# An attention and GEGLU block on one core: the output projection in plain F32 products with other load orders, and a third of the normalised input loaded into both halves of its tile at block changes

## The chip, the cores and the metric

The kernel runs on one core of one Trainium2 chip. The metric is the device time of one execution in microseconds (us). The engines are named as in the profile: PE (TensorE, matrix products; PEld is its weight load), DVE (VectorE), ACT (ScalarE), POOL (GpSimd) and SP (SyncE), which here issues every transfer.

## The reference

```
xn = layernorm(x)                                   # x: 2048 rows of 576, F32
q, k, v = xn @ wqkv                                 # 32 heads of 18
s = softmax(q k^T / sqrt(18)) v @ wo                # wo: 576 x 576
g = silu( (gelu(xn @ w_gate) * (xn @ w_up)) @ w_down )   # 4608 hidden
out = x + s * g
```

## The kernel before

[...] To keep the precision, an operand is split into a high part (rounded to fp32r) and a low part (what is left), and a product is the sum of high by high, high by low and low by high. The transposes of the prologue and the accumulation of the attention (L848) use plain F32 operands.

The order of the work on PE is written out by hand for the whole kernel; that of the other engines is given by a scheduler, except where `keep` (keep in program order) fixes it, and in the tail, where ACT, DVE and POOL follow the program as well. SP issues the transfers in its order, and eight of them can be open: a transfer is issued when the eighth before it has landed.

The 2048 rows of x are worked off in four blocks of 512 (`NB`, `TB`).

*Prologue* (to about 200 us). Layer norm, transposes and the projections to q, k and v for four blocks. Beside the last of them `wo` is read in five pieces, split by POOL (`split_wo`, L313) and stored in two parts, high and low, in the DRAM tile `wos` (`store_wo`, L321). The high and low parts of the transposed xn are stored in `xhs`.

*Main part* (to about 2456 us). The FFN runs in sections. A section forms one gate and one up product for 128 hidden channels and a block: 54 matmuls (L427) with the weights `wh`, `wl` (five buffers each, split from `raw`) and the block's `xd`. Each of the 18 rounds of a block has two sections, and a `down` of 42 matmuls (L538), which multiplies the activations (`ah`, `al`, their high and low parts, made by ACT and POOL from the sums `h`) by `T`, the prepared down weights, and adds the products to `M`. Between the matmuls of a section stand those of the attention: the scores for the maxima (L779, DVE), the scores again (L831), their exponential on ACT (L832) and the accumulation (L848).

*Block changes* (about 726, 1336 and 1942 us). A block's `xd` are six tiles of 128 partitions, `xd0` and `xd1` (the high and the low part) for each of three thirds k of xn's channels, XG = 3 groups of 64 channels to a tile. Both 64-partition halves of a tile hold the same data, since gate products use one half of the array and up products the other. In the last section of a block (`new` in `section`, L571) `load_xd` (L139) loads the first halves of thirds 0 and 1 by hooks in the section, and those of third 2 after it; `copy_xd` (L148) fills the second halves: those of `xd0` on ACT, those of `xd1` on POOL. POOL's order before is: the copies of third 0, the activation's sums, `ah`, `al`, the copies of third 1, `wh` and `wl`, the copies of third 2. `finish` puts the sums and cuts of that section into the tenth hook of the next one (`behind`, L640).

*Tail* (from about 2456 us). Five FFN sections and three downs are left, and the output projection in 16 steps, one for each 128 rows (`groups`). The order on PE: three sections, down 0, four steps, a section, three steps, down 1, two steps, a section, two steps, down 2, five steps. A step (`step`) is:

- `project`: attention rows by `wo`, five row groups (`NK`, the last of 64 rows) and two halves of 288 columns, in a PSUM slot of `ring`, which has three slots that sections, downs and steps share. With `oh`, `ol` and `woh`, `wol` these are 28 matmuls (L991).
- `multiply` (L995): the gate `yy` by the product, plus `xx`, and the store of the output rows.
- `split_o` for the step after the next: `oh` on ACT (L972), `ol` and a 64-partition piece of `oh` on DVE (L973, L974). After the last group of block 0 or 1 it also issues `load_o(b + 2)`, which reads the attention rows of a later block into the slots of `KA` that block b leaves (`OTS`).
- `gate` for the step after the next: tanh on ACT (L982) and one DVE operation (L983) on the FFN rows `ys`.
- `load_xy` four steps ahead, and two of the four `T` pieces of the next down, where there are any (`pieces`).

The attention rows that are not yet normalised at the end of the main part go through `load_scale`, `scale` (POOL, L705) and `store_scale` into `on`, one after the other. `XX` has three buffers and four more (`xxs`) later, `YY` has four.

```
for k in range(2):
    step()
load_raw(first + 4)
for k in range(2):
    step()
h, end = last_section("ring")
```

## Time and profile before

| | us |
|---|---|
| median of 3 runs | 2597.23 (2595.16 to 2600.65) |
| the profiled execution, its own time | 2595.73 |
| its span | 2593.9 |
| its granted PE clock | 0.995 |
| PE busy | 2554.1 |
| DVE busy | 2111.7 |
| POOL busy | 1599.7 |
| ACT busy | 1468.6 |

A row of a group reads: line, engine, operation, tiles (out<-in), shapes and count, then busy time and the mean of one in ns, then the idle time ahead of it and what ended it. Rows of the chain of waits are: start, length, engine, tile and line, with "x42" for 42 instructions in a row. A row of waits is: who waited, for whom, the time in all, how often, the longest. PE matmuls are pipelined, so the pace of a run of them (its length by its count) says more than the mean of one. The clock is that granted to PE, in parts of full speed.

```profile
PEclk9999999999999999999999999999999999999998
```

This line of the page is the granted clock in 40 equal slices of the span, in tenths of full speed.

### The profile page before, as it was taken

To read this page: it belongs to the slowest core of one execution; us is meant where nothing else is said; L and a number is where in the kernel's file an instruction comes from. 1 tells how busy PE (TensorE), PEld (TensorE's weight loads), DVE (VectorE), ACT (ScalarE), POOL (GpSimd) and SP (SyncE) were. 2 spreads that over 40 slices of the span, in tenths; PEclk is the share of its full clock that TensorE was granted. 3 is DMA by queue.
4 is the path that set the end of the run, shared out by engine and by line. 5 is a ranking of instruction groups with operands and counts; after the bars stand their busy time and mean duration, and the time that the engine had idled before them with its cause. 6 is when DMAs were issued, how large, how long until landed. Compare 5 with 4: busy or idle time off the path is not lost.

```text
span 2593.9 us, 52857 instructions
## 1 busy us (share of the span) xinstructions
PE 2554.1 (98%) x20548; PEld 1847.5 (71%) x20548; DVE 2111.7 (81%) x2399; ACT 1468.6 (57%) x1769; POOL 1599.7 (62%) x1679
## 2 busy tenths in 40 slices
PE   9999999999999999999999999999999999999988
PEld 8887766666666777666666676666666666676778
DVE  5325888888888888888878988888887888887377
ACT  3224366666666666555566655555566555556521
POOL 2115588888888855666667665555557655556641
PEclk9999999999999999999999999999999999999998
DMA  8865455555565566666666666666557665554683
GB/s 264 266 237 147 109 166 152 167 164 161 167 188 164 165 170 165 159 165 166 167 174 172 168 167 162 161 160 157 155 151 213 163 156 150 153 155 134 187 255 126
DMA packets 407880, 442.87 MB, mean 171 GB/s; under 512 B 106700, under 2 KB 286412, under 8 KB 407632
## 3 DMA queue, kind: packets, MB, share of 16 engines
q1 hardware_dynamic: 407632, 439.50, 61.6%
q8 instruction: 163, 2.67, 0.4%
q14 instruction: 85, 0.70, 0.1%
HBM read 344.12 MB, written 95.26 MB: 169 GB/s over the span
## 4 chain that ended last, share of the span: by engine, by line
PE 92%; DVE 2%; DMA 2%; POOL 1%; ACT 1%; issue 1%; SPq 1%; POOLq 0%; DVEq 0%; ACTq 0%
PE pg L427 27%; PE acc L848 17%; PE py L538 14%; PE pe L831 9%; PE pm L779 9%; PE po L187 7%; PE pu L427 7%; PE py L525 1%; PE po L991 1%; DMA raw<-in_B_w_up_dram 0%; DMA wol<-wos 0%; DVE mx L781 0%; DMA KA<-on 0%; PE pt L248 0%; DMA yy<-ys 0%
## 5 line engine op out<-in xcount | busy, mean ns | idle before, releaser
L832 ACT ACTIVATE pT<-pe 128x1024 f32<-128x1024 f32 x1024 | 1049.0, 1027 | 586.0 <-PE pe L831 551.1
L781 DVE TENSOR_REDUCE mx<-pm 128x2 f32<-128x1024 f32 x1024 | 1220.5, 1224 | 176.6 <-PE pm L779 161.8
L427 PE MATMUL pu<-xd,wh 64*128 64x512 f32 x2538 | 927.5, 397 | 6.5 <-POOL xd L153 4.9
L427 PE MATMUL pg<-xd,wh 64*128 64x512 f32 x2538 | 926.0, 396 | 1.9 <-ACT t L440 1.9
L427 PEld LDWEIGHTS pg<-xd,wh 64*128 64x128 f32 x2538 | 468.6, 185 | 123.7 <-issue 57.0
L427 PE MATMUL pg<-xd,wl 64*128 64x512 f32 x1269 | 496.4, 391 | 1.2 <-POOL wl L117 1.2
L427 PE MATMUL pu<-xd,wl 64*128 64x512 f32 x1269 | 495.9, 391 | 0.0
L427 PEld LDWEIGHTS pu<-xd,wh 64*128 64x128 f32 x2538 | 468.5, 185 | 24.4 <-POOL xd L153 5.7
L110 POOL TENSOR_SCALAR wh<-raw 128x384 fp32r<-128x384 f32 x402 | 215.4, 537 | 437.4 <-PE pu L427 333.4
L848 PE MATMUL acc<-pT,VS 128*32 128x512 f32 x4096 | 466.0, 595 | 0.0
L112 POOL TENSOR_TENSOR wl<-raw,wh 128x384 fp32r<-128x384 f32 x402 | 413.4, 1031 | 28.6
L779 PE MATMUL pm<-KA,QT 64*128 64x512 f32 x2048 | 416.5, 394 | 5.6 <-ACT pT L832 3.6
L831 PE MATMUL pe<-QT,KA 64*128 64x512 f32 x2048 | 412.5, 392 | 2.2 <-DVE mx L781 1.9
L538 PE MATMUL py<-T,ah 128*128 128x288 f32 x1876 | 385.9, 301 | 9.9 <-DVE yy L1000 7.0
L545 DVE TENSOR_TENSOR M<-py,M 128x576 f32<-128x576 f32 x448 | 338.8, 758 | 31.2 <-PE py L538 18.5
L538 PEld LDWEIGHTS py<-T,ah 128*128 128x128 f32 x1876 | 302.0, 190 | 65.9 <-issue 61.5
L456 POOL TENSOR_TENSOR al<-h,ah 128x512 fp32r<-128x512 f32 (+1 forms) x142 | 292.8, 2062 | 52.6 <-ACT ah L453 42.5
L848 PEld LDWEIGHTS acc<-pT,VS 128*32 128x32 f32 x4096 | 120.3, 109 | 276.5 <-issue 229.5
L538 PE MATMUL py<-T,al 128*128 128x288 f32 x938 | 277.8, 296 | 0.0
L831 PEld LDWEIGHTS pe<-QT,KA 64*128 64x128 f32 x2048 | 194.3, 184 | 113.0 <-DVE mx L781 26.2
L427 PEld LDWEIGHTS pg<-xd,wl 64*128 64x128 f32 x1269 | 234.4, 185 | 38.4 <-POOL wl L117 2.0
L427 PEld LDWEIGHTS pu<-xd,wl 64*128 64x128 f32 x1269 | 234.7, 185 | 8.3
(156 smaller groups left out, 2908.4 us busy)
## 6 DMA issues: line engine op xcount, KB each, us to landing
T<-ts SPq DMA_DIRECT2D x98, 576.0 KB
KA<-qk SPq DMA_DIRECT2D x768, 72.0 KB
T<-ts SPq DMA_DIRECT2D x98, 432.0 KB
raw<-in_B_w_gate_dram SPq DMA_DIRECT2D x144, 288.0 KB
raw<-in_B_w_up_dram SPq DMA_DIRECT2D x144, 288.0 KB
ts<-T SPq DMA_DIRECT2D x36, 576.0 KB
VS<-vs SPq DMA_DIRECT2D x128, 152.0 KB
qk<-t SPq DMA_DIRECT2D x72, 256.0 KB
```

What stands on the lines that cost most here:

```text
L110: first = nc.gpsimd.tensor_scalar(hi, raw, 1.0, 1.0, op0=ALU.mult, op1=ALU.mult)
L112: keep(nc.gpsimd.tensor_tensor(lo, raw, f(hi), op=ALU.subtract))
L187: nc.tensor.matmul(o, st, m, start=(i == 0), stop=(i == len(terms) - 1))
L427: nc.tensor.matmul(o, w[1 + wp][k][rr, c, :], xd[k][xp][rr, c, :], start=(i == 0), stop=(i == len(terms) - 1))
L456: keep(two.tensor_tensor(lo, raw, f(hi), op=ALU.subtract))
L538: nc.tensor.matmul(py[:, t, 0:DC], h[:, i, tt], T[:, w, k], start=n == 0, stop=n == 2)
L545: nc.vector.tensor_tensor(M[:, m], py[:, :, 0:DC], M[:, m], op=ALU.add)
L779: nc.tensor.matmul(pm[:, a], QS[u, r][rr, t * P:(t + 1) * P], KS[(u * NA + c) % KB][r][rr, :], start=True, stop=True)
L781: return nc.vector.tensor_reduce(MX[u][:, 2 * r:2 * r + 2, t, c], pm, axis=AX.X, op=ALU.max)
L831: nc.tensor.matmul(pe[:, a], KS[(u * NA + c) % KB][r][rr, t * P:(t + 1) * P], QS[u, r][rr, :], start=True, stop=True)
L832: nc.scalar.activation(PT[u, kt][:, 2 * r:2 * r + 2, :], pe, AF.Exp, scale=SCALE)
L848: nc.tensor.matmul(ACC[u][32 * a:32 * a + 32, :], VS[(u * NA + c) % VB][:, v:v + 32], pt[:, a, :], start=first, stop=last, skip_group_chec ...
```

## The change

*Output projection.* `split_wo`, `store_wo` and `wos` go. In the tail `wo` is read as it is into one F32 tile, and `project` multiplies the F32 rows in `KA` by it: ten products per step, five row groups by two halves. `split_o` goes. `XX` has five buffers (and the four `xxs`), `YY` seven; `load_x` and `load_y` ask for rows nine and seven groups ahead. The loads for the scaling are issued together, all four pieces of `T` for the next down are asked for ahead of the first step, the raw weights of the last section earlier, and `load_o(b + 2)` follows the products of the last step of block b. `gate` runs for the step after the next one, as before, with `step(False)` where a down stands between.

*Block changes.* `load_xd` takes `halves`; with 2 it issues a transfer for each half of a tile. The last third is loaded so, and its copies on ACT and POOL go. The POOL copies of thirds 0 and 1 stand together after the section, ahead of the sums; and `behind` issues sums and cuts at once, in program order, instead of in the tenth hook.

```diff
--- before.py
+++ after.py
@@ -92,7 +92,6 @@
     qk = dram.tile([2, 2 * D, S], F32, name="qk")
     vs = dram.tile([S, H, DH + 1], F32, name="vs")
     oT = dram.tile([NQ, P, S], F32, name="oT")
-    wos = dram.tile([2, D, D], F32, name="wos")
     rT = dram.tile([H, S], F32, name="rT")
     on = [dram.tile([D, TB], F32, name=f"on{b}") for b in range(NB)]
     mxT = [dram.tile([8 * QD, P], F32, name=f"mxT{i}") for i in range(2)]
@@ -136,12 +135,14 @@
         w[1].append(hi)
         w[2].append(lo)
 
-    def load_xd(b, k):
+    def load_xd(b, k, halves=1):
 
         out = []
         for i in range(2):
             t = wts.tile([P, XG, TB], F32R, name=f"xd{i}_{k}")
-            nc.sync.dma_start(f(t)[0:HR], xhs[b][i, k * XG * HR:(k + 1) * XG * HR, :].rearrange("(k p) t -> p k t", p=HR))
+            for a in range(halves):
+                nc.sync.dma_start(f(t)[HR * a:HR * a + HR],
+                                  xhs[b][i, k * XG * HR:(k + 1) * XG * HR, :].rearrange("(k p) t -> p k t", p=HR))
             out.append(t)
         return out
 
@@ -266,7 +267,6 @@
         nc.vector.memset(eps, EPS)
         for v in VN:
             nc.vector.memset(v, 1.0)
-        parts = []
         ORDER = (4, 5, 0, 1, 6, 7, 8, 2, 3)
         WQK, WV = {}, {}
 
@@ -309,18 +309,6 @@
             v = VN[2 * j + c]
             nc.scalar.activation(v[:, :, 1:DH + 1], o[:, 0:D // 2].rearrange("p (h d) -> p h d", d=DH), AF.Copy)
             nc.sync.dma_start(vs[t * P:(t + 1) * P, c * H // 2:(c + 1) * H // 2, :], v)
-
-        def split_wo(k):
-            n = min(P, D - k * P)
-            raw = raw_tile([P, D])
-            tc.keep_in_program_order(nc.sync.dma_start(raw[0:n], wo[k * P:k * P + n, :]))
-            hi, lo = (pro.tile([P, D], F32R, name=f"wo{i}", tag="rawp", bufs=5) for i in range(2))
-            split(hi[0:n], lo[0:n], raw[0:n])
-            return k, n, hi, lo
-
-        def store_wo(k, n, hi, lo):
-            for i, t in enumerate((hi, lo)):
-                tc.keep_in_program_order(nc.sync.dma_start(wos[i, k * P:k * P + n, :], f(t)[0:n]))
 
         NQT = 2 * D // P
         raw_v, ahead_qk, QR = [], [], []
@@ -372,10 +360,6 @@
                 if b == 0 and n in (7, 8):
                     split_wv(n - 7, raw_v[n - 7])
                 project(b, t, xt)
-                if b == NB - 1 and 2 <= n < NK + 2:
-                    store_wo(*parts.pop(0))
-                if b == NB - 1 and n < NK:
-                    parts.append(split_wo(n))
                 if n == 4 and b + 1 < NB:
                     norm(xr, b + 1)
             store_xt(b, xt)
@@ -612,11 +596,10 @@
         if g > 0 or n not in ATT:
             FF.pop("last", lambda: None)()
         if new:
-            xd.append(load_xd(b + 1, NG - 1))
-            for k in range(1, NG):
-                for i in range(XG):
-                    FF["hooks"].setdefault(7 * k + 2 * i - 5, []).append(lambda k=k, i=i: copy_xd(xd[k], 0, keep, i))
-            for k in range(NG):
+            xd.append(load_xd(b + 1, NG - 1, 2))
+            for i in range(XG):
+                FF["hooks"].setdefault(2 + 2 * i, []).append(lambda i=i: copy_xd(xd[1], 0, keep, i))
+            for k in range(NG - 1):
                 for i in range(XG):
                     copy_xd(xd[k], 1, keep, i)
             FF["xd"] = xd
@@ -638,10 +621,7 @@
             FF[ahead].setdefault(i, []).append(what)
 
         def behind(what):
-            if (n + 1) % (NR * G) == 0:
-                hook(9, lambda: what(keep))
-            else:
-                what(lambda i: i)
+            what(keep if (n + 1) % (NR * G) == 0 else lambda i: i)
 
         if g == 1 and (b, r + 1) in NEXT:
             load_rawd((r + 1) % NR)
@@ -937,64 +917,50 @@
 
 
     with tc.tile_pool(name="epi", bufs=1, reuse_waits="tile") as epi:
-        OW = [epi.tile([P, NK, D], F32R, name=name) for name in ("woh", "wol")]
-        XX = [epi.tile([P, D], F32, name=f"xx{i}") for i in range(3)]
-        YY = [epi.tile([P, D], F32, name=f"yy{i}") for i in range(4)]
-        OP = {}
+        OW = epi.tile([P, NK, D], F32, name="wo")
+        XX = [epi.tile([P, D], F32, name=f"xx{i}") for i in range(5)]
+        YY = [epi.tile([P, D], F32, name=f"yy{i}") for i in range(7)]
         groups = [(b, j) for b in range(NB) for j in range(TB // P)]
         rest, pieces = list(range(scaled, NU)), []
         pool, vec, act = nc.gpsimd, nc.vector, nc.scalar
         n = 0
 
         def load_wo():
-            nc.gpsimd.memset(f(OW[1])[HR:P, KT, :], 0.0)
-            for i, w in enumerate(OW):
-                nc.sync.dma_start(f(w)[:, 0:KT, :], wos[i, 0:R0, :].rearrange("(k p) n -> p k n", p=P))
-                for a in range(2 - i):
-                    nc.sync.dma_start(f(w)[HR * a:HR * a + HR, KT, :], wos[i, R0:D, :])
+            nc.sync.dma_start(OW[:, 0:KT, :], wo[0:R0, :].rearrange("(k p) n -> p k n", p=P))
+            nc.sync.dma_start(OW[0:HR, KT, :], wo[R0:D, :])
 
         def rows(k):
             b, j = groups[k]
             return slice(b * TB + j * P, b * TB + (j + 1) * P)
 
-        def load_xy(k):
+        def load_y(k):
+            if k < len(groups) and groups[k][0] < NB - 1:
+                nc.sync.dma_start(YY[k % len(YY)], ys[rows(k), :])
+
+        def load_x(k):
             if k < len(groups):
                 nc.sync.dma_start(XX[k % len(XX)], x[rows(k), :])
-                if groups[k][0] < NB - 1:
-                    nc.sync.dma_start(YY[k % 4], ys[rows(k), :])
-
-        def split_o(k):
-            if k >= len(groups):
-                return
-            b, j = groups[k]
-            oh, ol = OP[k] = [epi.tile([P, c, P], F32R, name=m, bufs=2) for m, c in (("oh", NK), ("ol", KT))]
-            raw = f(KA)[:, OTS[b]:OTS[b] + NK, j * P:(j + 1) * P]
-            act.activation(oh, raw, AF.Copy)
-            vec.tensor_tensor(ol, raw[:, 0:KT], f(oh)[:, 0:KT], op=SUB)
-            vec.tensor_tensor(oh[HR:P, KT, :], raw[0:HR, KT], f(oh)[0:HR, KT, :], op=SUB)
-            if b < 2 and j == TB // P - 1:
-                load_o(b + 2)
 
         def gate(k):
             if k < len(groups) and groups[k][0] < NB - 1:
-                yy = YY[k % 4]
+                yy = YY[k % len(YY)]
                 th = epi.tile([P, D], F32, name="th")
                 act.activation(th, yy, AF.Tanh, scale=0.25)
                 vec.scalar_tensor_tensor(yy, th, 1.0, yy, op0=ADD, op1=ALU.mult)
 
         def project(k):
+            b, j = groups[k]
             po = ring("po")
-            oh, ol = o = OP.pop(k)
-            terms = [(c, i, w) for c in range(KT) for i, w in ((0, 0), (0, 1), (1, 0))] + [(KT, 0, 0), (KT, 0, 1)]
             for c in range(2):
-                for m, (i, a, w) in enumerate(terms):
-                    nc.tensor.matmul(po[:, c, 0:DC], o[a][:, i, :], OW[w][:, i, DC * c:DC * c + DC], start=(m == 0),
-                                     stop=(m == len(terms) - 1))
+                for i in range(NK):
+                    rr = slice(0, P if i < KT else HR)
+                    nc.tensor.matmul(po[:, c, 0:DC], f(KA)[rr, OTS[b] + i, j * P:(j + 1) * P],
+                                     OW[rr, i, DC * c:DC * c + DC], start=i == 0, stop=i == KT)
             return po
 
         def multiply(k, po):
             b, j = groups[k]
-            xx, t = XX[k % len(XX)], YY[k % 4]
+            xx, t = XX[k % len(XX)], YY[k % len(YY)]
             t2 = t.rearrange("p (c d) -> p c d", c=2)
             if b < NB - 1:
                 vec.scalar_tensor_tensor(t2, t2, 0.25, po[:, :, 0:DC], op0=ALU.mult, op1=ALU.mult)
@@ -1005,16 +971,20 @@
             vec.tensor_tensor(xx, xx, t, op=ADD)
             nc.sync.dma_start(out[rows(k), :], xx)
 
-        def step():
+        def step(ahead=True):
             nonlocal n
             multiply(n, project(n))
-            split_o(n + 2)
-            gate(n + 2)
-            load_xy(n + 4)
+            b, j = groups[n]
+            if b < 2 and j == TB // P - 1:
+                load_o(b + 2)
             for t in pieces[:2]:
                 t()
             del pieces[:2]
+            load_y(n + len(YY))
+            load_x(n + len(XX))
             n += 1
+            if ahead:
+                gate(n + 1)
 
         def load_raw(n):
             FF["raw"][n] = load_gu(n % (NR * G))
@@ -1059,61 +1029,62 @@
         load_raw(first + 2)
         h, end = last_section("f")
         todo.pop("rec")[0]()
-        split_o(0)
+        for u in rest:
+            load_scale(u)
+        load_wo()
+        for k in range(2):
+            load_y(k)
+        load_raw(first + 3)
         end()
         sums_a(1, h, vec)
         cut_a(1, h, act, vec)
-        load_wo()
-        load_scale(rest[0])
-        load_xy(0)
-        load_xy(1)
-        load_raw(first + 3)
         h, end = last_section("ring")
-        split_o(1)
         end()
-        scale(rest[0])
-        store_scale(rest.pop(0))
-        if rest:
-            load_scale(rest[0])
-        load_xy(2)
+        for u in rest:
+            scale(u)
+            store_scale(u)
+        for k in range(4):
+            load_x(k)
+            load_y(k + 2)
         h1, end = last_section("f")
         last_down(0)
         end()
         gate(0)
-        while rest:
-            scale(rest[0])
-            store_scale(rest.pop(0))
-            if rest:
-                load_scale(rest[0])
+        gate(1)
         sums_a(0, h, pool)
         cut_a(0, h, pool, pool)
         sums_a(1, h1, pool)
         cut_a(1, h1, pool, pool)
-        gate(1)
+        load_raw(first + 4)
         for m in ("rawd", "tsum"):
             t = ffn.tile([P, 2, D], F32, name="xxs", tag=m)
             XX.extend((t[:, 0], t[:, 1]))
-        load_xy(3)
-        for k in range(2):
-            step()
-        load_raw(first + 4)
-        for k in range(2):
+        for t in pieces:
+            t()
+        del pieces[:]
+        for k in range(4, len(XX)):
+            load_x(k)
+            if k + 2 < len(YY):
+                load_y(k + 2)
+        for k in range(4):
             step()
         h, end = last_section("ring")
         end()
-        for k in range(3):
+        for k in range(2):
             step()
+        step(False)
         last_down(1)
+        gate(n + 1)
         sums_a(0, h, pool)
         cut_a(0, h, pool, pool)
-        for k in range(2):
-            step()
+        step()
         h, end = last_section("f")
         end()
         sums_a(1, h, vec)
         cut_a(1, h, act, vec)
         for k in range(2):
             step()
+        step(False)
         last_down(2, {6: ((vec, 6, SUB, 3),), 0: ((vec, 6, ADD, 0), (pool, 5, ADD, 0), (pool, 5, ADD, 2)),
                       4: ((vec, 6, SUB, 4), (vec, 4, ADD, 2)), 1: ((pool, 5, SUB, 1), (pool, 1, SUB, 3))})
         step()
```

## The prediction

> **What bounds the kernel now.** I read the page first, for the engine that fills the span, then the last stage as a table of stretches, then its waits, and last the chain of work at the three block changes.
>
> ```profile
> span 2593.9 us, 52857 instructions
> PE 2554.1 (98%) x20548; PEld 1847.5 (71%) x20548; DVE 2111.7 (81%) x2399; ACT 1468.6 (57%) x1769; POOL 1599.7 (62%) x1679
> ```
>
> PE is busy for 98% of the span, so time is won only where PE has less to do or stops waiting. The change touches two places: the tail, in which the output projection runs, and the block changes. The table below cuts the tail at the ends of its pieces of work; its columns are the stretch and its length, then busy time (instructions) of PE, PEld, DVE, ACT and POOL, the granted clock, the DMA share and GB/s.
>
> ```profile
> core 0: us, PE busy (x) PEld busy (x) DVE busy (x) ACT busy (x) POOL busy (x), PEclk, DMA share, GB/s
> 2456.30:2475.26 18.96, 18.96 (x164) 15.20 (x163) 11.74 (x14) 4.93 (x8) 6.67 (x9) 1.00 1.06 330
> 2475.26:2481.98 6.72, 6.14 (x43) 5.71 (x43) 6.63 (x11) 1.87 (x3) 1.30 (x1) 1.00 1.01 184
> 2481.98:2502.03 20.05, 16.75 (x114) 16.35 (x113) 15.29 (x18) 4.26 (x7) 16.13 (x15) 0.91 0.53 162
> 2508.38:2521.42 13.04, 11.57 (x86) 11.29 (x85) 6.56 (x11) 3.75 (x6) 3.32 (x5) 1.00 1.08 340
> 2521.42:2536.33 14.91, 8.78 (x44) 8.00 (x43) 13.16 (x17) 2.00 (x3) 5.18 (x5) 0.77 0.66 221
> 2557.72:2569.86 12.14, 8.94 (x44) 8.15 (x43) 11.34 (x18) 0.78 (x2) 1.28 (x1) 0.72 0.30 97
> 2569.86:2589.38 19.52, 19.36 (x142) 18.57 (x140) 17.31 (x25) 4.63 (x7) 5.82 (x4) 1.00 0.22 76
> ```
>
> The chain of waits prices undisturbed work, and names what the disturbed work waited for.
>
> ```profile
> 680.02 5.78 PE py L538 x42
> 2462.79 10.42 DMA wol<-wos
> 2499.29 10.31 DMA KA<-on
> 2511.53 8.04 DMA yy<-ys
> 2536.49 7.42 PE po L991 x56
> ```
>
> A down (42 matmuls of L538) costs 5.78 us, and a step of the projection, 28 of the 56 matmuls in the last row, 3.71 us. Against these, the rows of the table in order: three sections, no loss; down 0, 6.72 − 5.78 = 0.9; four steps, 20.05 − 4×3.71 = 5.2; three steps, 1.9; down 1, 9.1; down 2, 6.4; five steps, 1.0. In all 24.5 us in which PE waited, or ran at the 0.72 to 0.91 of its clock that the waiting stretches show. The waits of PE in the tail say on whom:
>
> ```profile
> PE py L538 <- DVE yy L1000: 7.0, 3, 4.7
> PE po L991 <- DVE ol L973: 4.9, 3, 3.3
> L973 DVE TENSOR_TENSOR ol<-KA,oh 128x512 fp32r<-128x512 f32 x16 | 14.9, 933 | 2.7 <-ACT oh L972 2.7
> ```
>
> The DVE is named, but its own predecessors in the chain are DMAs: the split weights (10.42 us), a block's rows of attention (10.31 us) and the FFN rows `ys` (8.04 us). So the loss has two roots, late loads and the low parts that DVE makes.
>
> **The change, part by part.**
>
> *Tail, the products.* 28 fp32r matmuls per step go, and 10 plain F32 products of 288 columns come. Nothing in the tail of before is such a product, but the accumulation of the attention is one.
>
> ```profile
> L848 PE MATMUL acc<-pT,VS 128*32 128x512 f32 x4096 | 466.0, 595 | 0.0
> 330.46 3.57 PE acc L848 x32
> ```
>
> The program issues 2048 of these products, and the trace has 4096 records: two per F32 product. Four stand side by side in the array (128*32), so 32 records take eight turns of 3.57/8 = 0.446 us for 512 columns. In proportion to columns a record of 288 takes 0.251 us, and a step of 20 records 5.02. [...] I take the middle, 5.16, since both rows are equally near: 16×(5.16 − 3.71) = **+23.2 us**, between +21.0 and +25.4. [...]
>
> *Tail, the waits.* What goes per step is one ACT activation, and on DVE the subtraction of 0.933 us at L973 with its small neighbour: 16×0.933 = 14.9 us of DVE, which stood ahead of the multiplies that free the ring slots. PE then reads the loaded rows themselves, so the 4.9 us row disappears by construction. The 7.0 us row ends at L1000, which waits for `yy`, that is for `gate` and its load. The new order asks for `ys` rows seven groups ahead and `x` rows nine ahead. `wo` is read once in its own form, half the bytes of `woh` and `wol`, and before the second of the five sections. Walking SP's new order by estimate, with the durations above (10.4 us for a large load behind others), the weights are there at about 2472, four steps' rows of `x` and `ys` before the first step, and all `T` pieces of down 1 at about 2492. `load_o(b+2)` now stands behind the PE products of the last step of block b, because PE reads the rows directly; before, it stood behind a split done two steps earlier. It is issued some two steps later, but 33 us of PE work lie between it and its first reader for b = 1 (a section of 18.96/3 = 6.3, three steps 15.5, a down 5.8, one step 5.2), and a section more for b = 0, against 10.3 for the load. That work covers it; without the cover it would cost up to those 10.3. The tightest is the last: the rows of block 3 and the `T` pieces of down 2, at about 2553 to 2554 for a PE that gets there at 2555. I leave 1 us of waiting: **−23.5 us**, between −24.5 and −13 if one wait of the size of a load stays.
>
> *Prologue.* Five loads, ten stores and five splits on POOL go from the last token block, which lies in the third of the page's forty slices.
>
> ```profile
> PE   9999999999999999999999999999999999999988
> ```
>
> PE is full there, so I take 0: these had PE's own work as cover. Two raw loads move ahead in SP's order, into the same cover.
>
> *Block changes.* Downs stand 33.3 us apart when nothing is in the way (680.02 to 713.33). The chain at the changes:
>
> ```profile
> 713.33 5.74 PE py L538 x42
> 751.29 5.74 PE py L538 x42
> 1319.86 5.74 PE py L538 x42
> 1360.41 5.81 PE py L538 x42
> 1925.35 5.74 PE py L538 x42
> 1961.61 5.74 PE py L538 x42
> ```
>
> The pairs that hold a change take 37.96, 40.55 and 36.26: 4.7, 7.2 and 3.0 us too much. What stood in the way:
>
> ```profile
> 726.57 7.71 DMA xd<-xhs
> 734.40 1.74 POOL xd L153 x3
> 741.28 2.91 POOL al L456
> 744.25 0.62 POOL xd L153
> PE pu L427 <- POOL xd L153: 3.6, 1, 3.6
> 1349.23 0.43 PE pu L427
> 1948.49 1.16 ACT xd L151 x2
> 1952.43 1.16 ACT xd L151 x2
> ```
>
> Change 1: a POOL copy of `xd` (744.25) had to wait behind the sums and the low part `al` (2.91 us), and PE behind it. This copy is of the last third, which the DMA now writes into both halves, so it goes; I take 2.3 of the 4.7 (0.5 to 3.3), as later DVE waits stay. Change 2: PE waited 3.6 us for a POOL copy behind `al`, and then ran matmuls at 0.43 instead of 0.23 for some 6 us. POOL's new order has the copies of the first two thirds ahead of the sums, so both go: 5.2 (2.8 to 6.1). Putting `sums` and `cut` in at once, not nine hooks later, delays only what stands behind them on POOL, the `wh` and `wl` splits of the next section, which have five buffers. Change 3: six copies stand on ACT between the exponentials that PE waits for; three of 0.58 go, 1.7 us.
>
> Against this stand two more DMAs at each change, in front of the `KA`, `VS`, raw and `T` loads in SP's queue, which the next down waits for.
>
> ```profile
> 1936.00:1947.00 11.00, 11.00 (x97) 6.92 (x95) 8.82 (x10) 9.69 (x12) 6.43 (x11) 1.00 1.02 212
> 1955.00:1959.00 4.00, 4.00 (x38) 2.91 (x38) 3.60 (x4) 3.44 (x5) 3.74 (x7) 1.00 1.03 410
> SPq L869 <- DMA xd<-xhs: 1.7, 1, 1.7
> ```
>
> While `xd` goes into 64 partitions the DMA engines are full at 212 GB/s; the `T` loads into 128 get 410. A transfer of a third is 64×3×512×4 = 393 KB, 1.9 us at 212 GB/s. Two more push the queue by 3.7 us if they run one behind the other, by nothing if the two halves share the time, as 410 GB/s would allow. I take 1.5 (0 to 3.7), hidden at changes 1 and 2, and charged fully to change 3, where `T` still moves at 1959 and the down starts at 1961.61: 1.7 − 1.5 = 0.2 (−2.3 to 1.8). The sum is 2.3 + 5.2 + 0.2: **−7.7 us**, between −11.2 and −1.0.
>
> [...]
>
> *Sum.* The profiled execution took 2595.73 us with a span of 2593.9. 2595.73 + 23.2 − 23.5 − 7.7 = 2587.7. The median of the runs shown, 2597.23, lies 1.5 above this execution; with it, **2589 us**. About 5 us (0.2%) is what a measurement of this kernel can tell from no change, so under 2592 counts as faster and over 2602 as slower.
>
> **The rivals.**
>
> *A: the doubled transfers push the `T` loads past their readers.* For it: the DMA share is 1.02 to 1.03 around the change, nothing there is idle, and 2.6 us after 1959 the down begins. Against: 212 GB/s is half of what the same engines do elsewhere. The price is the block changes' lower bound, −1.0 in place of −7.7: 2589 + 6.7 = 2596.
>
> *B: the F32 weight loads show.* Place: all 320 records of the projection.
>
> ```profile
> L848 PEld LDWEIGHTS acc<-pT,VS 128*32 128x32 f32 x4096 | 120.3, 109 | 276.5 <-issue 229.5
> L248 PE MATMUL pt<-ident,xx 128*128 128x128 f32 x80 | 9.4, 273 | 1.5 <-DVE xx L230 1.5
> ```
>
> The loads that are hidden in L848 have 32 columns, those of the projection 128. The transposes of L248 load 128 columns for each record and run at 9.4/80 = 0.117 us, so that is the most a load can hold PE: 320×0.117 = +37, 2589 + 37 = 2626. It decides from (2602 − 2589)/320 = 0.04 us a record. Against: 0.117 is well under the 0.251 of a record, and the fp32r loads of 128 columns are hidden behind passes of 0.1325. [...] No row of before shows a 128-column F32 load beside a long pass.
>
> *C: the tail's waits stay in part.* SP issues in order and the DMA share of the tail's first 19 us is already 1.06 at 330 GB/s; now `wo`, `ys` and scale loads are asked for together. If one load of 10.3 us stays late, 2589 + 9.5 = 2598; if all waits stay, 2612.
>
> *That the change doesn't do what it says* can't be for the products, which are in the program; for the loads it is C.
>
> **How the numbers follow.** Forecast 0.52, with a range of its own of 2582 to 2594 (from its terms: products −2.2 to +2.2, changes −3.5 to +3); A 0.17; C 0.18, of which a third over 2602; B 0.13. Faster than 2592: five sixths of the forecast and a fifth each of A and C, 0.50. Slower than 2602: B and a third of C, 0.19. Within: the rest, 0.31. The range 2577 to 2604 takes in A and the first case of C; B and the worst of C lie above it, all terms at their best below it, together about 0.2.
>
> **What would show it.** Steps: the chain should show 20 records of the projection in 5.0 to 5.3 us; 5.9 or more speaks for B. Tail: the waits of PE there should come to about 1 us, with the granted clock at 1.00 in every stretch; a wait ended by `KA<-on` or `T` would be C. Changes: downs 35.7, 35.4 and 36.1 us apart; 37 or more at all three is A, and then the `T` loads land after the sums are done. No wait on a POOL `xd` copy may be left at change 2. The prediction is wrong as a whole if F32 records cost over 0.3 us, or if the chain of the tail still runs through DMAs.

## The result, and the profile after

The changed kernel takes 2605.07 us in the median of 15 runs (2600.45 to 2608.41) against 2597.23 for the kernel before; the ratio is 1.0026, with a 95% interval of 1.0018 to 1.0034. It is slower by some 7 us, 0.26%, and the forecast was 2589. Its profiled execution took 2601.46 us, 5.7 more than that of before.

The page first. Its columns are those of the page of before.

```profile
span 2599.7 us, 52470 instructions
PE 2574.5 (99%) x20420; PEld 1842.9 (71%) x20420; DVE 2089.4 (80%) x2367; ACT 1452.6 (56%) x1744; POOL 1581.6 (61%) x1659
```

PE is busy for 20 us more, the span is 5.8 us longer: PE waits less and has more to do. The stretches of the tail, cut at the same pieces of work, show where.

```profile
core 0: us, PE busy (x) PEld busy (x) DVE busy (x) ACT busy (x) POOL busy (x), PEclk, DMA share, GB/s
2456.57:2475.17 18.60, 18.60 (x163) 15.10 (x163) 11.29 (x13) 3.62 (x5) 7.86 (x10) 1.00 0.97 277
2480.95:2503.04 22.09, 22.09 (x83) 13.75 (x83) 15.04 (x14) 3.42 (x5) 19.09 (x17) 1.00 0.93 301
2526.35:2532.13 5.78, 5.78 (x44) 5.78 (x44) 5.67 (x8) 0.00 (x0) 1.92 (x2) 1.00 0.60 194
2566.41:2594.71 28.30, 28.22 (x101) 17.30 (x100) 15.29 (x21) 2.74 (x4) 6.98 (x4) 1.00 0.11 42
```

PE is busy for the whole of each stretch and the clock is 1.00 throughout: down 1 takes 5.78 us where it took 14.91 before. No wait is left. But five steps of the projection take 28.30 us, 5.66 each, against a forecast of 5.16 and 3.71 before. The chain of waits has all steps, in five rows:

```profile
2480.95 22.09 PE po L957 x79
2509.45 16.90 PE po L957 x60
2532.13 5.19 PE po L957 x19
2543.74 16.90 PE po L957 x60
2566.41 28.23 PE po L957 x100
```

They sum to 89.3 us; 16 steps of 3.71 are 59.4. (The change also moved one step from behind down 1 to behind the section that follows, which the description of the change leaves out: 20 and 60 records stand there.) The products cost 29.9 us more, and the tail as a whole, from the end of the last down of the main part to the last product, went from 133.1 to 138.1 us: the waits gave back 24.9.

At the block changes, the chain has the downs around each change (the first, and the second after it). The last row of a view can be cut off by its end, as x33 and the last x41 are; its start counts here.

```profile
713.91 5.74 PE py L522 x42
785.55 4.55 PE py L522 x33
1317.53 5.74 PE py L522 x42
1346.76 8.73 DMA T<-ts
1355.53 7.14 PE py L522 x41
1390.20 5.74 PE py L522 x42
1922.17 5.74 PE py L522 x42
1994.46 5.61 PE py L522 x41
```

The waits of PE for `T`, one row from a window around change 2 and one from change 3:

```profile
PE py L522 <- DMA T<-ts: 2.8, 2, 2.2
PE py L522 <- DMA T<-ts: 2.7, 2, 2.3
```

The pairs of intervals are 71.64, 72.67 and 72.29 us, against 74.46, 73.91 and 69.54 before: 2.8 and 1.2 us gained at changes 1 and 2, 2.75 lost at change 3, 1.3 in all. The waits are new: at changes 2 and 3 the down waits 0.6 and 0.4 us for its first piece of `T`, does one matmul and waits another 2.2 and 2.3 us for a later piece. And once it had waited, it ran on slowly: 41 matmuls took 7.14 us at change 2, where 42 take 5.74. The granted clock (third column from the end) tells why:

```profile
1355.50:1357.00 1.50, 1.47 (x6) 1.47 (x7) 0.00 (x0) 0.00 (x0) 0.00 (x0) 0.50 0.58 152
1357.00:1359.00 2.00, 2.00 (x11) 2.00 (x10) 1.18 (x2) 0.00 (x0) 0.61 (x1) 0.55 0.34 123
1359.00:1361.00 2.00, 2.00 (x17) 2.00 (x17) 1.76 (x3) 0.00 (x0) 1.31 (x2) 1.00 0.50 148
```

For some 3.4 us behind the wait PE had about half of its full speed, which cost another 1.4 us.

### The profile page after: what moved, and what is told of

Same layout as the page of the kernel before. It is cut to its first block, busy times and chain, and to the rows that moved or that the text cites. A ratio compares the mean times of both kernels' runs of the same rounds, so it can differ in the third digit from the quotient of the medians.

```text
span 2599.7 us, 52470 instructions
## 1 busy us (share of the span) xinstructions
PE 2574.5 (99%) x20420; PEld 1842.9 (71%) x20420; DVE 2089.4 (80%) x2367; ACT 1452.6 (56%) x1744; POOL 1581.6 (61%) x1659
## 4 chain that ended last, share of the span: by engine, by line
PE 95%; DMA 2%; DVE 1%; POOL 1%; SPq 1%; ACT 1%; issue 0%; POOLq 0%; DVEq 0%; ACTq 0%
PE pg L411 26%; PE acc L828 17%; PE py L522 15%; PE pe L811 9%; PE pm L759 9%; PE pu L411 7%; PE po L188 7%; PE po L957 3%; PE py L509 1%; DMA T<-ts 1%; DMA raw<-in_B_w_up_dram 0%; PE pgu L411 0%; DVE mx L761 0%; DMA xd<-xhs 0%; PE pt L249 0%
## 5 line engine op out<-in xcount | busy, mean ns | idle before, releaser
L411 PEld LDWEIGHTS pu<-xd,wh 64*128 64x128 f32 x2538 | 467.5, 184 | 18.2 <-DVE t L425 2.9
```

What stands on the lines that cost most here:

```text
L411: nc.tensor.matmul(o, w[1 + wp][k][rr, c, :], xd[k][xp][rr, c, :], start=(i == 0), stop=(i == len(terms) - 1))
```

## The experiments

All are timed in five rounds beside the kernel before. The ratio is to that kernel, in the same session. The diffs below show the core of each edit; where lines between are left out stands "...". They are against the changed kernel, but for that of e12_old_loads, against the kernel before, and that of e9_parts_on_pool, against e6_parts_new_loads.

| run | median, us | before beside it | ratio (95%) |
|---|---|---|---|
| e1_pad | 2593.52 | 2598.96 | 0.9981 (0.9972 to 0.9990) |
| e2_half_switches | 2598.97 | 2598.96 | 1.0001 (0.9992 to 1.0010) |
| e3_changes_as_before | 2602.64 | 2598.96 | 1.0017 (1.0008 to 1.0025) |
| e4_both_halves | 2677.54 | 2598.96 | 1.0303 (1.0289 to 1.0317) |
| e5_pad_t_first | 2583.72 | 2596.92 | 0.9950 (0.9937 to 0.9962) |
| e6_parts_new_loads | 2600.45 | 2596.92 | 1.0012 (1.0003 to 1.0020) |
| e7_pad_stored_twice | 2585.94 | 2596.92 | 0.9962 (0.9949 to 0.9974) |
| e8_pad_order_only | 2586.38 | 2596.92 | 0.9963 (0.9950 to 0.9977) |
| e9_parts_on_pool | 2590.22 | 2597.73 | 0.9968 (0.9955 to 0.9980) |
| e10_both | 2583.41 | 2597.73 | 0.9945 (0.9932 to 0.9957) |
| e11_tail_as_before | 2590.11 | 2597.73 | 0.9968 (0.9956 to 0.9981) |
| e12_old_loads | 2590.55 | 2597.73 | 0.9976 (0.9967 to 0.9985) |

### Why a step takes 5.6 us

The timeline of the weight loads of the changed kernel, from the first product of a step on, gave the lead. The bracket is the idle time ahead of a row.

```profile
2509.38 1.75 PEld L957 LDWEIGHTS po<-wo,KA 128*128 128x128 f32 x8 [0.35 <-issue]
2511.52 0.29 PEld L957 LDWEIGHTS po<-wo,KA 64*128 64x128 f32 x2 [0.39 <-issue]
2512.20 1.75 PEld L957 LDWEIGHTS po<-wo,KA 128*128 128x128 f32 x8 [0.39 <-issue]
2514.33 0.29 PEld L957 LDWEIGHTS po<-wo,KA 64*128 64x128 f32 x2 [0.39 <-issue]
```

The form is the rows by the columns of the array that a product uses. Within eight records of the form 128*128 the loads follow each other without a gap. Ahead of the two records of the fifth row group, which has 64 rows and so the form 64*128, and again behind them, there is a gap of 0.39 us in which nothing shows. From the start of one matmul to the start of the next it is 0.2425 us inside a form, and four intervals of 0.333 to 0.347 around each pair of borders, so a border costs some 0.2 us.

**e1_pad**: multiply the fifth group over 128 rows, with zeros in the upper half of `wo`.

```diff
-                    rr = slice(0, P if i < KT else HR)
-                    nc.tensor.matmul(po[:, c, 0:DC], f(KA)[rr, OTS[b] + i, j * P:(j + 1) * P],
-                                     OW[rr, i, DC * c:DC * c + DC], start=i == 0, stop=i == KT)
+                    nc.tensor.matmul(po[:, c, 0:DC], f(KA)[:, OTS[b] + i, j * P:(j + 1) * P],
+                                     OW[:, i, DC * c:DC * c + DC], start=i == 0, stop=i == KT)
...
+            nc.gpsimd.memset(OW[HR:P, KT, :], 0.0)
```

> The fifth row group is multiplied over 128 rows, the upper 64 of wo being zero, so all ten products of a step have the form 128*128. Theory (the change of form between 128*128 and 64*128 costs time: intervals of 0.333 to 0.347 us around it, 0.2425 elsewhere): every interval becomes 0.2425, a step 20 x 0.2425 = 4.85 instead of 5.64, and the whole 16 x 0.79 = 12.6 us shorter than the changed kernel, about 2592. Rival (an F32 product has a fixed cost that the accumulation of the attention does not show): the step stays at 5.6 and the time within 2 us of the changed kernel.

**e2_half_switches**: all 128-row products of a step first, the two of 64 rows behind them.

```diff
-            for c in range(2):
-                for i in range(NK):
+            for i, c in [(i, c) for c in range(2) for i in range(KT)] + [(KT, 0), (KT, 1)]:
```

> The same ten products of a step, but the two of the 64-row group stand side by side at the end, so the form changes twice per step instead of four times. Theory (the change of form costs, not the row count): half the loss, some 0.4 us a step, 6 us shorter than the changed kernel. Rival (a product over 64 rows is itself slow): the four records over 64 rows keep their 0.34 us and the time does not move by over 1 us.

In e1_pad the loads of the same place stand in one row, in e2_half_switches there are two borders to a step; below the timelines are the chains of three steps, first of e1_pad, then of e2_half_switches.

```profile
2511.10 5.15 PEld L957 LDWEIGHTS po<-wo,KA 128*128 128x128 f32 x22 [0.35 <-issue]
```

```profile
2511.63 3.69 PEld L956 LDWEIGHTS po<-wo,KA 128*128 128x128 f32 x16 [0.35 <-issue]
2515.70 0.78 PEld L956 LDWEIGHTS po<-wo,KA 64*128 64x128 f32 x4 [0.39 <-issue]
2516.87 0.30 PEld L956 LDWEIGHTS po<-wo,KA 128*128 128x128 f32 x2 [0.38 <-issue]
```

```profile
2511.17 14.75 PE po L957 x60
```

```profile
2511.70 15.72 PE po L956 x60
```

A step takes 4.92 us padded (4.85 without the fixed part at the start of a run of steps), 5.24 with half the borders, 5.63 with all. Against the changed kernel's ratio, e1_pad is 0.0045 lower, 11.7 us, and e2_half_switches 0.0025, 6.5 us, where 12.6 and 6 were expected. In the profiled executions the tail, 138.1 us in the changed kernel, is 126.9 in e1_pad and 131.8 in e2_half_switches. Padding executes more zeros and is faster; four records over 64 rows side by side cost no more than others: the 15.72 − 14.75 = 0.97 us between the two chains is what the five borders inside three steps cost, at 0.2 each. So it is the change of form that costs here, and not the row count nor a price of F32 products in general. What happens inside the gap at a border the trace doesn't show.

### What happened to the waits of the tail

**e12_old_loads**: the kernel before with its order of loads, buffers and block changes, but padded F32 products and no low parts. `wo` is read once, as it is. Of its diff, the part at the end of a step:

```diff
-            split_o(n + 2)
+            b, j = groups[n]
+            if b < 2 and j == TB // P - 1:
+                load_o(b + 2)
             gate(n + 2)
             load_xy(n + 4)
```

> The kernel before with the padded plain F32 products of e1_pad and without the low parts, but with its own order of loads, its three xx and four yy buffers and its block changes; load_o follows the products. Steps of 4.85 instead of 3.71, +18.2 us. Theory (the waits of the tail before came from DVE, which made the low parts, not from late loads): the waits of PE in the tail fall under 4 us and the time is 2592 to 2598. Rival (late loads were the larger root, as the prediction had it): waits of 8 us or more stay, for yy or the loads, 2602 or longer.

**e6_parts_new_loads**: the opposite, the changed kernel's order of loads with the 28 products of before and `split_o`. It has three `xx` and four `yy` buffers, so rows are asked for seven and four groups ahead, not nine and seven.

```diff
             multiply(n, project(n))
+            split_o(n + 2)
-            b, j = groups[n]
+            b, j = groups[min(n + 2, len(groups) - 1)]
             if b < 2 and j == TB // P - 1:
                 load_o(b + 2)
```

> The new order of loads in the tail and the new block changes, but the projection of the kernel before: high and low parts, wo split in the prologue, 28 fp32r products a step (three xx and four yy buffers for want of space, so rows are asked for seven and four groups ahead). Theory (of the 24.5 us lost in the tail of before the larger part was late loads): steps of 3.71 us, the waits of PE in the tail fall from 14.5 us to under 7, 12 to 18 us under the kernel before. Rival (DVE with the low parts was the bound, some 4.1 us of DVE work a step against 3.71 of PE): the waits for DVE stay at 10 us or more and the time is within 8 us of the kernel before.

The waits of PE in the tail, first of the kernel before the two rows that the prediction doesn't show, then of e12_old_loads all there are, then of e6_parts_new_loads the four largest:

```profile
PE py L538 <- DVE M L545: 2.2, 2, 1.3
PE py L538 <- DVE h L1046: 0.4, 1, 0.4
```

```profile
PE py L520 <- DVE M L527: 0.6, 1, 0.6
```

```profile
PE po L989 <- DVE ol L980: 8.6, 5, 2.4
PE po L989 <- DVE h L1049: 3.5, 1, 3.5
PE py L540 <- DVE M L547: 2.2, 2, 1.3
PE po L989 <- DMA wol<-wos: 1.6, 1, 1.6
```

With the old loads and no low parts 0.6 us of waits remain of 14.5; with the new loads and the low parts 15.9 us stand in these four rows. The tail as a whole says the same: 132.8 us in e6_parts_new_loads against 133.1 before, and 127.6 in e12_old_loads against 126.9 in e1_pad. With either kind of products the new order of loads is worth under a microsecond, so late loads were not the root of the loss. The work of DVE is the likely one. By the mean durations of the groups of before, a step of the first twelve groups has 4.1 us of work for DVE (0.93 and 0.41 for the low parts, 1.01 for the gate, 0.75 and about 1.0 for the product and the sum), against 3.71 of PE; to this come the sums of the sections and downs.

```profile
L974 DVE TENSOR_TENSOR oh<-KA,oh 64x128 fp32r<-64x128 f32 x16 | 6.5, 408 | 0.4
L983 DVE SCALAR_TENSOR_TENSOR yy<-th,yy 128x576 f32<-128x576 f32 x12 | 12.1, 1009 | 10.4 <-ACT th L982 10.2
L1000 DVE SCALAR_TENSOR_TENSOR yy<-yy,po 128x576 f32<-128x576 f32 x12 | 9.0, 748 | 3.4 <-PE po L991 3.4
```

e12_old_loads takes 1.3 us of that away and also makes a step 1.14 us longer for PE; how much of the relief comes from which, no run tells. The rival of e6_parts_new_loads held; it came out 0.0012 over the kernel before, part of it the late `T` at its block changes (2.1 us of wait at each of changes 2 and 3). e12_old_loads came out 1.5 us better than the range expected.

**e9_parts_on_pool**: as e6_parts_new_loads, block changes as in e5_pad_t_first below, but most low parts made by POOL.

```diff
-            vec.tensor_tensor(ol, raw[:, 0:KT], f(oh)[:, 0:KT], op=SUB)
-            vec.tensor_tensor(oh[HR:P, KT, :], raw[0:HR, KT], f(oh)[0:HR, KT, :], op=SUB)
+            (vec if k < 4 else pool).tensor_tensor(ol, raw[:, 0:KT], f(oh)[:, 0:KT], op=SUB)
+            (vec if k < 2 else pool).tensor_tensor(oh[HR:P, KT, :], raw[0:HR, KT], f(oh)[0:HR, KT, :], op=SUB)
```

> As e6_parts_new_loads (28 fp32r products a step, new loads), with the raw loads behind the T loads at block changes as in e5_pad_t_first, and with the low parts of the attention rows made by POOL from the fifth group on (the 64-row piece from the third) instead of DVE. Theory (in e6 DVE was the bound of the tail: 8.6 us of waits for ol, 7.7 us for other DVE work): the waits for ol fall under 3 us, all waits of PE in the tail under 8 us; with 4.85 - 3.71 = 1.14 us less a step than the padded F32 products this comes out at 2575 to 2584, at or under e5_pad_t_first. Rival (POOL is too slow or too busy with the sums of the last sections): PE waits for POOL's ol instead, 10 us or more of waits, 2588 or longer.

The waits of PE in its tail:

```profile
PE po L995 <- POOL oh L987: 11.3, 1, 11.3
PE po L995 <- POOL ol L986: 3.6, 2, 2.5
```

The rival held: one wait of 11.3 us for the third group's piece, which stood behind the sums and cuts of the last sections on POOL. Its tail is 132.0 us, five more than with the padded products: here the cheaper products did not pay, since the low parts waited in POOL's queue.

### What the block changes are worth

**e3_changes_as_before**: the changed kernel with `load_xd`, the copies and `behind` of the kernel before.

```diff
-            xd.append(load_xd(b + 1, NG - 1, 2))
+            xd.append(load_xd(b + 1, NG - 1))
...
-            for k in range(NG - 1):
+            for k in range(NG):
```

> The new tail with the block changes of the kernel before (third 2 of xd loaded once and copied, POOL order and hooks as before). Theory (the doubled transfers make the T loads late and give back nearly all that the copies' removal brings): the downs at the changes stand 37.9, 40.5 and 36.3 us apart, no wait of PE for T, and the whole is within 1.5 us of the changed kernel. Rival (block changes are better by 5 or more, and all the loss is in the tail): 5 us or more slower than the changed kernel.

The ratio is 0.0009 under that of the changed kernel, 2.3 us, with intervals that overlap. The block changes of the change give nothing that can be measured; that they cost 2 us is not shown. The pairs of downs vary by more than that from run to run: e1_pad and e2_half_switches have the changed kernel's block changes, and their three pairs sum to 219.4 and 218.5 us, against 216.6 in the changed kernel and 217.9 in the kernel before. In e3_changes_as_before change 1 and 3 came as expected (37.3 and 36.3 us), but for a wait of 0.7 us for `T` at change 3; change 2 took 39.4, a microsecond less than before.

**e5_pad_t_first**: e1_pad, and the raw weights at a block change are asked for in the eighteenth hook, behind the `T` loads.

```diff
+        def ask(i):
+            FF["raw"][i] = load_gu(i % (NR * G))
+
         for i in range(n + 1, min(n + 3, NF)):
             if i not in FF["raw"]:
-                FF["raw"][i] = load_gu(i % (NR * G))
+                if n % (NR * G) == 0 and n > 0:
+                    hook(17, lambda i=i: ask(i))
+                else:
+                    ask(i)
```

> The padded projection of e1_pad, and at block changes the raw weight loads are issued behind the four T loads instead of ahead of them (two transfers of 295 KB, some 2.6 us). Theory (the doubled transfers of xd only hurt because T stands behind them in SP's queue): T lands 2 to 3 us earlier after the preceding down, the waits of PE for T at changes 2 and 3 (2.8 and 2.7 us in the changed kernel) fall under 0.5 us, and the whole is 4 to 6 us shorter than e1_pad, some 10 us under the kernel before. Rival (the transfers are late because the DMA engines are full, whatever the order): the waits stay over 2 us, or raw is late instead and PE waits for wh.

Its downs around changes 2 and 3:

```profile
1318.66 5.74 PE py L522 x42
1387.12 5.74 PE py L522 x42
1920.10 5.74 PE py L522 x42
1988.19 5.74 PE py L522 x42
```

68.46 and 68.09 us, 4.2 less than in the changed kernel at each; no wait for `T` is left there. Putting `T` ahead of the raw weights was enough, and the rival didn't come. It gained 0.0031 on e1_pad, 8 us, more than expected: in e1_pad the two changes had waits for `T` of 3.4 and 3.9 us, and each cost another 1.5, for the slow matmuls behind it (41 in 7.19 and 7.24 us). Against the kernel before the three pairs are 2.2, 5.5 and 1.5 us shorter, 9.1 in all.

**e8_pad_order_only**: e1_pad with the last third loaded once and copied, but with POOL's new order.

```diff
-            xd.append(load_xd(b + 1, NG - 1, 2))
+            xd.append(load_xd(b + 1, NG - 1))
...
+            for i in range(XG):
+                FF["hooks"].setdefault(9 + 2 * i, []).append(lambda i=i: copy_xd(xd[2], 1, keep, i))
```

> The padded projection of e1_pad; at block changes the last third is loaded once and copied as in the kernel before (three more ACT copies, three more POOL copies behind al), but POOL keeps the new order, thirds 0 and 1 ahead of the sums. Theory (the gain of the block changes is POOL's order, the doubled transfer gives it back): no wait for T, change 2 within 3.5 us of an undisturbed pair of downs, change 3 as before at 36.3, change 1 between 36 and 38; 2 to 4 us shorter than e1_pad. Rival (the copies of the last third are what costs): PE waits for a copy of xd at changes 1 and 2 as before and the time is that of e1_pad or longer.

Change 2 takes 69.9 us for the pair, the first intervals of changes 1 and 3 are 37.3 and 36.2: as expected, and 0.0018 under e1_pad, 4.7 us, a little more than the range. Both have POOL's new order, so this difference is what the doubled transfer costs while `T` stands behind it, less what it saves in copies. What POOL's order brings is read against the kernel before: the three pairs of e8_pad_order_only are 4.6 us shorter, about half of the 9.1 of e5_pad_t_first, and nearly all of it at change 2. No wait for `T` shows in e8_pad_order_only; the other 4.5, some 1.5 at each change, are then what the doubled transfer brings once `T` is not late. That last step is worked out, not run by itself.

**e4_both_halves** and **e7_pad_stored_twice** asked what sets the pace of the doubled transfer. The first, against the changed kernel, reads each row group twice in one transfer with a repeated source; the second, with the padded products, stores the last third twice in the prologue and reads it as 128 partitions.

```diff
+            for g in range(XG * (halves - 1)):
+                both = rows[g * HR:g * HR + HR].rearrange("(o p) t -> o p t", o=1).to_broadcast([2, HR, TB])
+                nc.sync.dma_start(f(t)[:, g], both)
```

> The changed kernel, but the two halves of the last third are written by one transfer over 128 partitions for each 64-row group (three per tile, six per change) instead of one per half (four). [...] Rival (the source side or the number of packets sets the pace): they land no earlier and the time stays.

```diff
+                nc.sync.dma_start(f(t), xh2[b][i].rearrange("k a p t -> (a p) k t"))
...
+                for a in range(2 * (b > 0)):
+                    for k in range(2):
+                        keep(nc.sync.dma_start(xh2[b][i, k, a], f(xt[i])[HR * k:HR * k + HR, KT - 1]))
+                    keep(nc.sync.dma_start(xh2[b][i, 2, a], f(xt[2])[HR * i:HR * i + HR, :]))
```

> The padded projection of e1_pad; the prologue stores the last third of xn twice, so that at a change one transfer per tile fills all 128 partitions (2 transfers of 786 KB instead of 4 of 393 KB, the same bytes). Theory (a transfer into 64 partitions runs at half the pace): the two land within 4.2 us instead of 6.6, T 2 to 3 us earlier, its waits under 0.5 us, and 4 to 7 us shorter than e1_pad, less some 1 us for 18 more stores in the prologue. Rival (the pace is set by the bytes or by the memory): 6.6 us as before, no gain.

Stretches at change 2 of e4_both_halves, while those transfers run, and the last third's transfers at change 3 of e5_pad_t_first (64 partitions each) and of e7_pad_stored_twice (128):

```profile
1364.00:1384.00 20.00, 8.64 (x68) 6.45 (x66) 8.11 (x7) 8.08 (x10) 10.22 (x10) 0.81 0.13 52
```

```profile
1940.10:1946.30 6.20, 5.29 (x45) 4.05 (x43) 4.25 (x5) 5.87 (x8) 5.89 (x8) 1.00 0.96 214
```

```profile
1940.30:1944.50 4.20, 4.10 (x36) 3.25 (x32) 3.25 (x4) 3.87 (x7) 4.02 (x6) 1.00 0.85 290
```

e4_both_halves, expected 4 to 7 us under the changed kernel by an estimate from the 410 GB/s of the `T` loads, missed its question: with the repeated source the DMA share, a mean over 16 engines, is 0.13, about two engines' worth, and 52 GB/s, and PE waits 16.2 us for `xd` at that change. e7_pad_stored_twice answers it: counted from the landing of the transfer ahead of them, the same bytes land in 4.2 us instead of 6.2, as the theory had it. The transfers into the halves run one behind the other, in a stretch of 214 GB/s: in the changed kernel the four of change 3 land at 1944.1, 1945.8, 1947.5 and 1948.8 us, by their semaphores in the trace. At changes 2 and 3 of e7_pad_stored_twice waits for `T` of 1.6 and 0.8 us are left, more than expected.

**e10_both** joins e5_pad_t_first and e7_pad_stored_twice; **e11_tail_as_before** puts the block changes of e5_pad_t_first alone into the kernel before.

> e5_pad_t_first with the last third of xn stored twice in the prologue and loaded by one transfer per tile (e7_pad_stored_twice). Theory (with T ahead of raw the transfers of xd are hidden already): T lands 2 us earlier still, but nothing waits for it, so within 1.5 us of e5_pad_t_first. Rival (the earlier KA, VS and raw loads are worth something): 2 us or more shorter.

> The kernel before, prologue and tail untouched, with the block changes of e5_pad_t_first (doubled transfers, POOL order of the change, raw behind T). Theory (the block changes are worth what the downs show: 2 us at change 1, 5 and 1.5 at the others, once T is not late): 7 to 9 us under the kernel before, and then the padded tail alone is the rest, 4 to 6 us, of what e5_pad_t_first gains. Rival (what the changes gain is lost again as waits in the main part): under 4 us.

e10_both is within the interval of e5_pad_t_first: once `T` is ahead, nothing waits for what the faster transfer brings. e11_tail_as_before is 8.3 us under the kernel before, all from block changes. Of the 13 us by which e5_pad_t_first beats the kernel before, the padded tail is then 5; its own tail in the profile, 127.0 against 133.1, has it at 6. e5_pad_t_first and e10_both are the fastest runs, 13 and 14 us under the kernel before; no more was tried.

## Why the prediction was wrong

**The products**, forecast at +23.2 us (21.0 to 25.4), measured +29.9. The step that failed is "a step of 20 records": it took all twenty to be alike, and priced them by rows in which nothing changes its form. Four of the twenty stand over 64 rows, and each crossing between 128*128 and 64*128 costs some 0.2 us; the sum had no term for it. The price of a record was wrong too, the other way: the padded step takes 4.85, below the lower bound of 5.02 as well as the middle of 5.16. A record of 288 columns takes 0.2425 us, less than its share of the accumulation's 0.446 for 512 columns (0.251). No run shows the step of 5.30 on which the upper end, +25.4, and the middle of 5.16 rest: it was the author's estimate, and the runs showed 4.85 where all records have one form. The records alone would have cost 16 × (4.85 − 3.71) = 18.2, 5.0 under the forecast, and the crossings 11.7 more; that the two partly cancel is luck. The sign for this term was not met either way: a step of 5.63 lies between the 5.0 to 5.3 of the forecast and the 5.9 of rival B.

The kernel before avoided the crossings: there the upper 64 rows of its fifth group held the low part, so all 28 products had one form. And the profile of before showed the price, behind each down, where a gate product of the form 64*128 follows one of 128*128, here behind the down at 713.33 in the chain of waits:

```profile
719.07 0.42 PE pg L427
```

The products of a section follow each other at 0.23 us; here 0.2 us are lost. In the changed kernel a gap of 0.39 us stands ahead of the weight loads at each border, and e1_pad and e2_half_switches put the cost of its 64 borders at 12 us.

**Rival B**, weight loads that show, named the right place and the wrong cause: 128-column F32 loads are hidden within one form (no gap in 22 loads of e1_pad). At a border the loads' engine stands idle, for 0.39 us; whether a load is what PE waits for there is not shown.

**The waits of the tail**, forecast at −23.5, measured −24.9: the size was right and its reason half wrong. The step that failed is "the loss has two roots, late loads and the low parts": e12_old_loads, with the old order of loads, has 0.6 us of waits, and e6_parts_new_loads, with the new one and the low parts, has a tail as long as that of before. The chain of before ran through the `wol`, `KA` and `yy` loads, and the prediction took what a chain passes through for what a change there would free. **Rival C** didn't come.

**The block changes**, forecast at −7.7, measured −1.3 in the profiled execution (+1.4 and +0.5 in e1_pad and e2_half_switches, with the same block changes). What was to be gained was right: with `T` on time, in e5_pad_t_first, the three changes gain 2.2, 5.5 and 1.5 us, where 2.3, 5.2 and 1.7 were forecast, and the waits for POOL's copies are gone. The step that failed is "I take 1.5 (0 to 3.7), hidden at changes 1 and 2, and charged fully to change 3", the cost of the doubled transfers. It was 4.2 us at change 2 and 4.2 at change 3, by the same pairs of downs. The two halves' transfers run one behind the other, and `T` lands some 3.3 us later after the preceding down at change 3. Of the 4.2 us, 2.8 and 2.7 are waits and the rest is the half clock behind them (0.50 at both), for which the sum had no term.

**Rival A** came true in its mechanism and its size (−1.0), at changes 2 and 3. Its sign did not show it: by the first matmul of each down the intervals are 34.9, 35.5 and 35.3 us, near or under the 35.7, 35.4 and 36.1 forecast, since the waits stand behind that matmul. (The lower bound of change 3 should be 1.7 − 3.7 = −2.0, not −2.3.)

That the doubled transfer might cost nothing, the lower end of "0 to 3.7", was the author's estimate, from the 410 GB/s of the `T` loads. The paces were 290 GB/s into 128 partitions in e7_pad_stored_twice against 214 into 64 in e5_pad_t_first; but two transfers issued one after the other did not run at the same time: the four of change 3 landed 1.7, 1.7 and 1.3 us apart in the changed kernel.

**The sum.** From 2587.7 forecast for the profiled execution to 2601.46 are 13.8 us: 6.7 from the products, 6.4 from the changes, −1.4 from the waits, and 2 in places that the change hardly touches (0.5 of it ahead of the first down, 0.5 behind the last product).

## What to carry to other kernels

Price a product by its form in the array and by that of its neighbours: a last row group of 64 among groups of 128 cost more here than its zeros would, 5.63 us a step against 4.92. Where a chain runs through loads, add up what the engine behind them has to do in a step first; if that is more than the step, as the 4.1 us against 3.71 here, earlier loads may gain nothing. Transfers added ahead of others in a queue delayed them here by their whole length, some 3.3 us for the two at change 3; to reorder what stands behind them was enough to take the cost away. And count a wait inside a dense run of matmuls with the slow stretch that may follow it: here 1.4 us behind a wait of 2.2, nothing behind one of 1.6.

## What was not expected of the hardware

A wait of 2.2 us behind the first matmul of a down was followed by some 3.4 us at a granted clock of 0.50 to 0.55, and 41 matmuls took 7.14 us, so the wait cost more than half as much again. The waits of 2.1 us in e6_parts_new_loads were followed by the same pace (41 matmuls in 7.26 and 7.24 us); that of 1.6 us in e7_pad_stored_twice was not:

```profile
1353.88 5.67 PE py L528 x41
```

A transfer whose source repeats 64 rows twice ran at 52 GB/s with a DMA share of 0.13 in e4_both_halves; the transfers into 64 partitions of e5_pad_t_first ran at 214 GB/s with a share of 0.96.
